# Turned down-projection with delayed scatter in a fused attention and mixture-of-experts kernel

## The chip, the cores and the metric

The kernel runs on one core of a Trainium2 chip. The metric is the device time of one execution in microseconds. A core has TensorE (PE; its weight loads are listed as PEld), VectorE (DVE), ScalarE (ACT), GpSimd (POOL) and SyncE (SP). In this kernel SP issues direct DMAs and POOL issues indirect ones (gathers and scatters); each of these engines works through its own queue in order.

## The reference

```
scores = z z^T / S                       # B = 8, S = 2496, d_qk = 64
attn   = max(scores, 0)^2
x      = u * (attn v)                    # (19968, 256) rows
logits = x @ w_gate                      # 8 experts
e      = argmax(logits)                  # one expert per row
gate   = softmax(logits)[e]
out    = gate * (max(x @ w1[e], 0) @ w2[e])   # w1: 256 x 1024, w2: 1024 x 256
```

Everything is fp32. The kernel splits each operand into a high part, in the form that PE takes (fp32r), and a low rest (hi and lo), and adds three products: hi hi, hi lo, lo hi.

## The kernel before

The first part (to about 1305 us) is attention over eight batches, five chunks of columns each. It leaves the rows x in DRAM (xrows), and for every expert a list of entries (gate and row number) in DRAM (lst), which the routing scatters there.

The second part works through tiles. A tile is a block of rows of one expert: four, three or two blocks of 128 rows. `order` holds 47 tiles, 31 of four blocks, 4 of three and 12 of two (11 further two-block tiles run only if the counts need them; with these inputs they do not). NM is 47. The last three tiles in the order have four, three and two blocks.

For each tile, by name in the code:

- `load_e` gathers the tile's entries (gate, row number) into a buffer `ent`, of which there are 6 (POOL).
- `load_x` gathers the rows x themselves, one indirect DMA per block (POOL).
- `turn_x` transposes them: DVE transposes within 32 x 32 blocks (L742), SP writes the result to DRAM (L745) and reads it back in four pieces (L747), which puts the blocks where they belong. `split_x` makes hi and lo of it (L757 on ACT, L758 on DVE).
- The hidden size 1024 is cut into 8 pieces of 128 (a two-block tile takes two pieces at once, so it has 4 groups; the others have 8). A group is one step of the loop in `tiles`.
- `up` (L775): the hidden tile of a group, six matmuls per piece, weights w1 standing, x moving, up to 512 columns. ACT takes the Relu to hh (L779), DVE makes the rest hl (L780).
- `down` (L796, L798): the rows of y. For each block s of the tile, hh[:, s] stands in PE and w2 moves, hi and lo of w2 side by side (512 columns); then hl[:, s] stands and the hi part of w2 moves (256 columns). y of a tile lies in PSUM, two blocks to a buffer of tag ps2, of which there are two; so a tile of three or four blocks takes both.
- `finish` (L806, L807, L809): per block ACT multiplies the second half of y by the gate, DVE multiplies the first half by the gate and adds; then POOL scatters the block's rows to the output.
- `load_w` gathers the weights of the next tiles' experts (POOL, L681), `split_piece` makes hi and lo of them (ACT L731 and L733, DVE L732 and L734), in rings of tag t4.

In the loop of `tiles`, `up` runs two groups ahead of `down`, and the loads three to four tiles ahead. The order of instructions on each engine is set by a planner in the tile framework, which simulates the timeline and may move instructions ahead of others. What is wrapped in `pinned(...)` comes, on each engine, behind all that was written before it. In before, `finish` is not pinned.

The buffers with the names u, x and x1 belong to the attention part (`gate_x`), one of each; after attention they are free.

Of the kernel before, what the change touches and what calls it, by code (L numbers as in the profile page):

```python
# [8 lines left out]
F32 = mybir.dt.float32  # L9
# [10 lines left out]
P = 128  # L20
KQ = 64
G, R = 4, 32
D = 256
E = 8
F = 1024
QC = 512
ENT, PAD = 16, 12
# [21 lines left out]
def fused_kernel(ctx: ExitStack, tc: tile.TileContext, zt, ut, v, wg, wcat, out):  # L49
    nc = tc.nc  # L50
# [13 lines left out]
    BS, SS = BIG // P, SMALL // P  # L64
# [3 lines left out]
    dram = ctx.enter_context(tc.tile_pool(name="dram", bufs=1, space=DRAM))  # L68
    ps2 = ctx.enter_context(tc.tile_pool(name="ps2", bufs=2, space=PSUM))
    ps1 = ctx.enter_context(tc.tile_pool(name="ps1", bufs=3, space=PSUM))  # L70
    psm = ctx.enter_context(tc.tile_pool(name="psm", bufs=1, space=PSUM))
    sb = ctx.enter_context(tc.tile_pool(name="sb", bufs=1))
# [5 lines left out]
    def ring2():  # L78
        return sb.tile([P, QC], FR, name="t2", tag="t2", bufs=10)

    def ring_f():
        return sb.tile([P, 2, QC], F32, name="tf", tag="tf", bufs=3)
# [280 lines left out]
    def pinned(work):  # L363

        last = {}
        for i in nc.cur_bb.bb.instructions[-400:]:
            last[i.engine] = i
        with ExitStack() as behind:
            for i in last.values():
                behind.enter_context(tc.issue_after(i))  # L370
            work()
# [278 lines left out]
    NF = F // P  # L650
# [12 lines left out]
    NM = len(order)  # L663
# [6 lines left out]
    blocks = [k for _, _, k in order]  # L670
# [3 lines left out]
    lists, ents, xgs, pieces, turned, xts, yts = {}, {}, {}, {}, {}, {}, {}  # L674
    outs, kept = [], []

    def load_w(w, h):
        which, t, _ = order[first_of[w]]
        wr = slot(free[0])
        free.append(free.pop(0))  # L680
        nc.gpsimd.indirect_dma_start(out=wr, out_offset=None, in_=wcat,  # L681
                                     in_offset=bass.IndirectOffsetOnAxis(ap=lists[which]["widx"][:, h, t:t + 1], axis=0))
        weights[w, h] = wr
# [2 lines left out]

    def load_e(i):
        which, t, k = order[i]
        en = ents[i] = sb.tile([P, BS, ENT], F32, name="ent", bufs=6)
        to = en.rearrange("p s w -> p (s w)")  # L690
        eidx = lists[which]["eidx"]
        parts = [(by4, t, 0, BS)] if k == BS else [(by2, t, 0, 2)]
        if k == 3:
            parts.append((lst, eidx.shape[1] - N3 + t - 2 * ND - NB, 2, 3))
        for src, at, a, z in parts:
            d = nc.gpsimd.indirect_dma_start(out=to[:, a * ENT:z * ENT], out_offset=None, in_=src,
                                             in_offset=bass.IndirectOffsetOnAxis(ap=eidx[:, at:at + 1], axis=0))
            if which == "A":
                firsts.append(d)
                for of, o in scatters:  # L700
                    if of == B - 1:
                        tc.declare_no_dep(d.ins, o.ins, reason="places of a later batch")

    def token(i, s):
        return bass.IndirectOffsetOnAxis(ap=ents[i].bitcast(I32)[:, s, 1:2], axis=0)

    def load_x(i):
        which, t, k = order[i]
        src = xrows[0:NTOK - S, :] if which == "A" else xrows
        xg = ring_rows()  # L710
        for s in range(k):
            nc.gpsimd.indirect_dma_start(out=xg[:, s, :], out_offset=None, in_=src, in_offset=token(i, s))  # L712
        xgs[i] = xg
# [37 lines left out]
    def split_x(i):  # L751

        k = blocks[i]
        tp = turned.pop(i).rearrange("p (a j t) -> p j a t", a=G, t=R)
        xh, xl = [x.rearrange("p i n -> p (i n)")[:, 0:k * D] for x in (ring_hi(), ring_lo())]
        h, l = [x.rearrange("p (j a t) -> p j a t", a=G, t=R) for x in (xh, xl)]
        nc.scalar.copy(h, tp)  # L757
        nc.vector.tensor_tensor(l, tp, h.bitcast(F32), op=ALU.subtract)  # L758
        xts[i] = [x.rearrange("p (i n) -> p i n", i=2) for x in (xh, xl)]

    def up(gi):
        i, g = groups[gi]
        n = blocks[i] * P
        w1 = pieces[piece_of[gi]][0]
        xh, xl = xts[i]
        ph = ps1.tile([P, QC], F32, name="ph", tag="ps1")
        m = fs_of[i]
        for c in range(m):
            f = g * m + c
            fs = slice(f % 2 * P, (f % 2 + 1) * P)  # L770
            o = ph[:, c * n:(c + 1) * n]
            p = 0
            for dd in range(2):
                for part, xx in ((0, xh), (0, xl), (1, xh)):
                    nc.tensor.matmul(o, lhsT=w1[:, part, dd, fs], rhs=xx[:, dd, :n], start=p == 0, stop=p == 5)  # L775
                    p += 1
        hh, hl = ring2(), ring2()
        m *= n
        nc.scalar.activation(hh[:, :m], ph[:, :m], AF.Relu)  # L779
        nc.vector.scalar_tensor_tensor(hl[:, :m], ph[:, :m], 0.0, hh[:, :m].bitcast(F32),  # L780
                                                     op0=ALU.max, op1=ALU.subtract)
        return hh, hl

    def down(gi, hh, hl):
        i, g = groups[gi]
        k = blocks[i]
        n = k * P
        w2 = pieces[piece_of[gi]][1]
        if g == 0:
            yts[i] = [ps2.tile([P, 2, QC], F32, name=f"y{s}", tag="ps2") for s in range(-(-k // 2))]  # L790
        for s in range(k):
            for c in range(fs_of[i]):
                f = g * fs_of[i] + c
                y = yts[i][s // 2][:, s % 2, :]
                cs = slice(c * n + s * P, c * n + (s + 1) * P)
                nc.tensor.matmul(y, lhsT=hh[:, cs], rhs=w2[:, f % 2].rearrange("p i d -> p (i d)"),  # L796
                                 start=f == 0, stop=False)
                nc.tensor.matmul(y[:, 0:D], lhsT=hl[:, cs], rhs=w2[:, f % 2, 0, :], start=False, stop=f == NF - 1)  # L798

    def finish(i):  # L800
        which, t, k = order[i]
        yo = ring_f().rearrange("p a (b d) -> p (a b) d", d=D)
        for s in range(k):
            y = yts[i][s // 2][:, s % 2, :]
            gate = ents[i][:, s, 0:1]
            nc.scalar.mul(yo[:, s, :], y[:, D:2 * D], gate)  # L806
            nc.vector.scalar_tensor_tensor(yo[:, s, :], y[:, 0:D], gate, yo[:, s, :], op0=ALU.mult, op1=ALU.add)  # L807
        for s in range(k):
            d = nc.gpsimd.indirect_dma_start(  # L809
                out=out, out_offset=token(i, s),  # L810
                in_=yo[:, s, :], in_offset=None, bounds_check=NTOK - 1, oob_is_err=False)
            for o in outs:
                tc.declare_no_dep(d.ins, o.ins, reason="rows are distinct")
            outs.append(d)
        del ents[i]
# [50 lines left out]
    for b in range(B):  # L866
        for c in range(NC_):
# [9 lines left out]
            f, z = {0: (-NKP * 4 + 1, 4), 1: (-NKP * 4 + 1, 4), 2: (-NKP * 4 + 1, 4), 3: (-NKP * 5 + 4, 7), 4: (-NKP * 4, 3)}[c]  # L877
# [12 lines left out]
    for work in (lambda: split_v(0, 0), lambda: split_z(0, 1), lambda: split_z(0, 2), lambda: prepare(0),  # L890
                 lambda: prepare(1), lambda: split_v(0, 1), lambda: split_z(0, 3), lambda: prepare(2)):
        pinned(work)
    bg.extend([nothing] * 2 + [constants])
    later = []
    loads = {2 * NKP - 2: [lambda: load_e(0)],
             2 * NKP - 3: [lambda: load_e(1)],
             NKP + 4: [lambda: load_x(0)],
             NKP + 3: [lambda: load_e(2)],
# [9 lines left out]
    for s, (b, c, kp) in enumerate(steps):  # L908
# [34 lines left out]
        if s == LAST:  # L943
            hs = {0: up(0)}
# [15 lines left out]

    def tiles(lo, hi, n_pieces):

        mine = [gi for gi, (i, _) in enumerate(groups) if lo <= i < hi]
        for gi in mine:
            i, g = groups[gi]
            G = NF // fs_of[i]
            if bg:
                pinned(bg.pop(0))
            if g == 0:
                for w, h in ((wof[i] + 1, 1), (wof[i] + 2, 0)):  # L970
                    if own[i] and w <= wof[hi - 1]:
                        load_w(w, h)
                if i + 3 < hi:
                    load_x(i + 3)
                if i + 4 < hi:
                    load_e(i + 4)
            ahead = min(gi + LU, mine[-1])
            while n_pieces < min(piece_of[ahead] + LP + 1, NPC * (wof[hi - 1] + 1)):
                split_piece(n_pieces)
                n_pieces += 1  # L980
            if i + 2 < hi and g == G // 2:
                turn_x(i + 2)
            if i + 1 < hi and g == G - 3:
                pinned(lambda: split_x(i + 1))
            if gi + LU <= mine[-1]:
                hs[gi + LU] = up(gi + LU)
            down(gi, *hs.pop(gi))
            if g == G - 1:
                finish(i)

    tiles(0, NM, n_pieces)
    needed = nc.values_load(lists["F"]["ns"], min_val=0, max_val=NS)

# [56 lines left out]
```

## Time and profile before

| | us |
|---|---|
| runs | 2232.24, 2224.86, 2226.58 |
| median | 2226.58 |
| profiled execution | 2225.69 |
| span of the profiled execution, first to last instruction | 2223.9 |

| engine | busy us | share of the span |
|---|---|---|
| PE | 2197.9 | 99% |
| PEld | 1854.1 | 83% |
| DVE | 1678.0 | 75% |
| ACT | 1313.2 | 59% |
| POOL | 697.4 | 31% |

All figures come from one profiled execution. Durations of matmuls overlap, since they are pipelined and their ends are modelled. The chain of waits follows the work that ended last back from the last instruction. Idle time of an engine counts only where another one waits for it.

### The profile page before, as it was taken

How to read it: one execution, taken by the hardware profiler on the slowest of the kernel's cores; microseconds unless marked ns; L12 is line 12 of the kernel's file. 1: busy time of each engine (PE TensorE's matmuls, PEld its weight loads, DVE VectorE, ACT ScalarE, POOL GpSimd, SP SyncE). 2: the span in 40 equal slices, each digit the busy share in tenths (PEclk: the TensorE clock that was granted, in tenths of full speed). 3: DMA queues.
4: the chain of work that ended last, by engine and by line, in shares of the span. 5: the costliest groups of instructions: out<-in, count | busy, mean ns of one | idle time of the engine just before them, and what ended most of it. 6: DMA issues, size and time to landing. Idle time of an engine off the chain costs nothing.

```text
span 2223.9 us, 32938 instructions
## 1 busy us (share of the span) xinstructions
PE 2197.9 (99%) x11664; PEld 1854.1 (83%) x11664; DVE 1678.0 (75%) x2782; ACT 1313.2 (59%) x1808; POOL 697.4 (31%) x720
## 2 busy tenths in 40 slices
PE   9999999999999999999999999999999999999997
PEld 6888888888888888888888888888888888888886
DVE  9888888888888888888888787566565575666653
ACT  8658657657667667667577544445454454554543
POOL 3010220220220220310222644455455455555521
PEclk9999999999999999999999999999999999999998
DMA  7966867858868758768857884565465465656530
GB/s 248 260 174 219 240 154 234 233 153 246 223 166 242 222 151 256 209 165 255 214 148 219 221 265 146 160 193 167 148 215 184 151 209 175 199 164 218 170 106 23
DMA packets 271884, 430.64 MB, mean 194 GB/s; under 512 B 109099, under 2 KB 167152, under 8 KB 252256
## 3 DMA queue, kind: packets, MB, share of 16 engines
q1 hardware_dynamic: 239200, 308.92, 48.8%
q0 software_dynamic: 32512, 119.55, 16.9%
q8 instruction: 93, 1.52, 0.3%
q14 instruction: 79, 0.65, 0.1%
HBM read 262.68 MB, written 166.20 MB: 193 GB/s over the span
## 4 chain that ended last, share of the span: by engine, by line
PE 90%; DVE 3%; DMA 2%; issue 2%; ACT 1%; POOL 1%; SPq 0%; POOLq 0%; DVEq 0%; ACTq 0%
PE ph L775 17%; PE acc L359 15%; PE acc L356 15%; PE acc L358 15%; PE y L796 12%; PE y L798 6%; PE ps_s L321 4%; PE ps_s L322 4%; PE pt L411 1%; DMA scr<-s 1%; DMA rows<-xrows,ent 1%; POOL out_dram L809 0%; POOL rows L712 0%; DVE tlo L335 0%; ACT tf L329 0%
## 5 line engine op out<-in xcount | busy, mean ns | idle before, releaser
L480 POOL DMA_INDIRECT lst<-gw,posi x160 | 201.3, 1258 | 872.0 <-DVE posi L477 535.6
L359 PE MATMUL acc<-thi,t 128*128 128x512 f32 (+1 forms) x1200 | 461.3, 386 | 0.0
L356 PE MATMUL acc<-thi,t 128*128 128x512 f32 (+1 forms) x1200 | 450.5, 386 | 0.6 <-DVE thi L333 0.6
L358 PE MATMUL acc<-tlo,t 128*128 128x512 f32 (+1 forms) x1144 | 443.0, 387 | 1.1 <-DVE tlo L335 1.1
L780 DVE SCALAR_TENSOR_TENSOR t<-ph,t 128x512 fp32r<-128x512 f32 (+1 forms) x328 | 220.0, 672 | 227.5 <-ACT t L779 223.6
L779 ACT ACTIVATE t<-ph 128x512 fp32r<-128x512 f32 (+1 forms) x328 | 192.8, 588 | 334.8 <-PE ph L775 304.2
L796 PE MATMUL y<-t,t 128*128 128x512 f32 x1062 | 378.6, 396 | 1.4 <-DVE tf L807 1.4
L775 PE MATMUL ph<-thi,t 128*128 128x512 f32 (+2 forms) x1248 | 375.6, 360 | 0.5 <-DVE t L780 0.3
L329 ACT ACTIVATE tf<-ps_s 128x1024 f32<-128x1024 f32 (+2 forms) x240 | 229.0, 962 | 184.4 <-PE ps_s L322 184.0
L798 PE MATMUL y<-t,t 128*128 128x256 f32 x1062 | 290.0, 281 | 2.6 <-DVE t L780 2.6
L356 PEld LDWEIGHTS acc<-thi,t 128*128 128x128 f32 x1200 | 225.3, 188 | 41.7 <-DVE thi L333 1.1
L359 PEld LDWEIGHTS acc<-thi,t 128*128 128x128 f32 x1200 | 225.3, 188 | 39.5
L775 PEld LDWEIGHTS ph<-thi,t 128*128 128x128 f32 x1248 | 225.5, 189 | 37.5 <-DVE t L780 1.9
L358 PEld LDWEIGHTS acc<-tlo,t 128*128 128x128 f32 x1144 | 214.9, 188 | 40.6 <-DVE tlo L335 3.4
L330 ACT ACTIVATE tf<-tf 128x1024 f32<-128x1024 f32 (+2 forms) x240 | 237.1, 998 | 5.9
L796 PEld LDWEIGHTS y<-t,t 128*128 128x128 f32 x1062 | 197.9, 188 | 43.2 <-DVE tf L807 1.9
L268 DVE STREAM_TRANSPOSE s<-tf 128x1024 f32<-128x1024 f32 x160 | 197.0, 1233 | 45.1 <-ACT tf L330 44.9
L775 PE MATMUL ph<-tlo,t 128*128 128x512 f32 (+2 forms) x624 | 224.7, 360 | 2.2 <-DVE tlo L758 2.2
L809 POOL DMA_INDIRECT out_dram<-tf,ent x160 | 166.5, 1041 | 191.6 <-DVE tf L807 151.2
L798 PEld LDWEIGHTS y<-t,t 128*128 128x128 f32 x1062 | 200.4, 189 | 13.9 <-DVE t L780 2.9
L712 POOL DMA_INDIRECT rows<-xrows,ent x160 | 164.6, 1029 | 105.1 <-DMA ent<-lst,lfeidx 60.5
L335 DVE TENSOR_TENSOR tlo<-tf,thi 128x1024 fp32r<-128x1024 f32 (+1 forms) x168 | 190.7, 1138 | 9.0 <-ACT thi L333 8.6
(237 smaller groups left out, 3929.8 us busy)
## 6 DMA issues: line engine op xcount, KB each, us to landing
scr<-s SPq DMA_DIRECT2D x80, 1024.0 KB
s<-scr SPq DMA_DIRECT2D x320, 256.0 KB
vr<-in_v_dram SPq DMA_DIRECT2D x80, 256.0 KB
u<-in_ut_dram SPq DMA_DIRECT2D x32, 512.0 KB
xrows<-th SPq DMA_DIRECT2D x128, 128.0 KB
far<-th SPq DMA_DIRECT2D x31, 512.0 KB
th<-far SPq DMA_DIRECT2D x124, 128.0 KB
lst<-pad SPq DMA_DIRECT2D x16, 624.0 KB
```

The costliest lines, as they stand in the source:

```text
L268: nc.vector.transpose(out=to, in_=a.rearrange("p i (t s k) -> p i t s k", t=4, s=G))
L329: nc.scalar.activation(a[:, :, m:n], ps[:, :, m:n], AF.Relu)
L330: nc.scalar.activation(a[:, :, m:n], a[:, :, m:n], AF.Square)
L356: nc.tensor.matmul(acc[d][:, :n], lhsT=vh, rhs=hi[:, i, :n], start=first and i == 0, stop=False)
L358: nc.tensor.matmul(acc[d][:, :n], lhsT=vh, rhs=lo[:, i, :n], start=False, stop=False)
L359: nc.tensor.matmul(acc[d][:, :n], lhsT=vl, rhs=hi[:, i, :n], start=False, stop=last and i == 1)
L480: i = nc.gpsimd.indirect_dma_start(out=lst, out_offset=bass.IndirectOffsetOnAxis(ap=posi[:m, j:j + 1], axis=0), in_=gw[:m, j, :], in_offse ...
L775: nc.tensor.matmul(o, lhsT=w1[:, part, dd, fs], rhs=xx[:, dd, :n], start=p == 0, stop=p == 5)
L779: nc.scalar.activation(hh[:, :m], ph[:, :m], AF.Relu)
L780: nc.vector.scalar_tensor_tensor(hl[:, :m], ph[:, :m], 0.0, hh[:, :m].bitcast(F32), op0=ALU.max, op1=ALU.subtract)
L796: nc.tensor.matmul(y, lhsT=hh[:, cs], rhs=w2[:, f % 2].rearrange("p i d -> p (i d)"), start=f == 0, stop=False)
L798: nc.tensor.matmul(y[:, 0:D], lhsT=hl[:, cs], rhs=w2[:, f % 2, 0, :], start=False, stop=f == NF - 1)
```

## The change

Tiles of three and four blocks, other than the last three tiles of the order, become "flat": 33 of 47.

- Their down-projection turns its operands round. For each half h of the 256 output columns the slice of w2 stands in PE and the hidden tile moves with all its columns (512 or 384): w2 hi with hh, w2 hi with hl, w2 lo with hh. y comes out with output columns on partitions and rows along the free side, and takes one ps2 buffer.
- `turn_y`, behind the tile's last group, turns it back as `turn_x` does: DVE transposes within 32 x 32 blocks from PSUM into x1, SP writes that to DRAM and reads it back in four pieces into u or x in turns.
- `finish` of a flat tile runs eight groups later, pinned: per block one multiply by the gate on ACT, then the scatters.
- There are 9 entry buffers in place of 6.

The other 14 tiles keep the form of before.

```diff
 def load_e(i):
-        en = ents[i] = sb.tile([P, BS, ENT], F32, name="ent", bufs=6)
+        en = ents[i] = sb.tile([P, BS, ENT], F32, name="ent", bufs=9)
...
+    def flat(i):
+        return blocks[i] != SS and i < NM - 3
...
         if g == 0:
-            yts[i] = [ps2.tile([P, 2, QC], F32, name=f"y{s}", tag="ps2") for s in range(-(-k // 2))]
+            if flat(i):
+                yts[i] = ps2.tile([P, 2, QC], F32, name="y", tag="ps2")
+            else:
+                y2 = [ps2.tile([P, 2, QC], F32, name=f"y{s}", tag="ps2") for s in range(-(-k // 2))]
+                yts[i] = [y2[s // 2][:, s % 2, :] for s in range(k)]
+        if flat(i):
+            for h in range(2):
+                ds_ = slice(h * P, (h + 1) * P)
+                y = yts[i][:, h, :n]
+                wh, wl = w2[:, g % 2, 0, ds_], w2[:, g % 2, 1, ds_]
+                nc.tensor.matmul(y, lhsT=wh, rhs=hh[:, :n], start=g == 0, stop=False)
+                nc.tensor.matmul(y, lhsT=wh, rhs=hl[:, :n], start=False, stop=False)
+                nc.tensor.matmul(y, lhsT=wl, rhs=hh[:, :n], start=False, stop=g == NF - 1)
+            return
...
+    def turn_y(i):
+        k = blocks[i]
+        sq = sb.tile([P, 2, QC], F32, name="x1").rearrange("p i n -> p (i n)")
+        nc.vector.transpose(out=sq[:, 0:k * D].rearrange("p (a s i e) -> p i s a e", a=G, s=k, i=2),
+                            in_=yts[i][:, :, 0:k * P].rearrange("p i (s a e) -> p i s a e", a=G, s=k))
+        far = dram.tile([P, F], F32, name="fary", tag="fary", bufs=4)
+        nc.sync.dma_start(far[:, 0:k * D], sq[:, 0:k * D])
+        tps[0] += 1
+        tp = sb.tile([P, 2, QC], F32, name="yt", tag="ux"[tps[0] % 2]).rearrange("p i n -> p (i n)")[:, 0:k * D]
+        for a in range(G):
+            nc.sync.dma_start(tp[a * R:(a + 1) * R].rearrange("p (g e) -> p g e", g=G),
+                              far[:, a * k * 2 * R:(a + 1) * k * 2 * R].rearrange("(g p) e -> p g e", g=G))
+        yts[i] = tp.rearrange("p (g s i e) -> p s i g e", g=G, s=k, i=2)
...
     def finish(i):
...
+            if flat(i):
+                nc.scalar.mul(yo[:, s, :].rearrange("p (i g e) -> p i g e", i=2, g=G), yts[i][:, s], gate)
+                continue
+            y = yts[i][s]
             nc.scalar.mul(yo[:, s, :], y[:, D:2 * D], gate)
             nc.vector.scalar_tensor_tensor(yo[:, s, :], y[:, 0:D], gate, yo[:, s, :], op0=ALU.mult, op1=ALU.add)
...
             down(gi, *hs.pop(gi))
+            if due and gi == due[0][0]:
+                pinned(lambda: finish(due.pop(0)[1]))
             if g == G - 1:
-                finish(i)
+                if flat(i):
+                    turn_y(i)
+                    due.append((gi + 8, i))
+                else:
+                    finish(i)
```

## Rows read from the trace of the kernel before

**Rows 1.** The page's part 1: busy time, share of the span, instructions of each engine.
```profile
PE 2197.9 (99%) x11664; PEld 1854.1 (83%) x11664; DVE 1678.0 (75%) x2782; ACT 1313.2 (59%) x1808; POOL 697.4 (31%) x720
```

**Rows 2.** The page's part 4, the chain that ended last, by engine and by line.
```profile
PE 90%; DVE 3%; DMA 2%; issue 2%; ACT 1%; POOL 1%; SPq 0%; POOLq 0%; DVEq 0%; ACTq 0%
PE ph L775 17%; PE acc L359 15%; PE acc L356 15%; PE acc L358 15%; PE y L796 12%; PE y L798 6%; PE ps_s L321 4%; PE ps_s L322 4%; PE pt L411 1%; DMA scr<-s 1%; DMA rows<-xrows,ent 1%; POOL out_dram L809 0%; POOL rows L712 0%; DVE tlo L335 0%; ACT tf L329 0%
```

**Rows 3.** Stretches: length; busy (x) of PE, PEld, DVE, ACT, POOL; clock; DMA share; GB/s.
```profile
400.00:600.00 200.00, 200.00 (x1056) 166.23 (x1055) 168.90 (x288) 131.72 (x153) 38.11 (x44) 1.00 0.75 212
...
1306.00:2210.00 904.00, 897.23 (x4843) 773.88 (x4842) 568.33 (x994) 442.60 (x812) 434.69 (x417) 1.00 0.53 168
```

**Rows 4.** The same stretch, first instructions on tile y alone, then line L775 alone.
```profile
1306.00:2210.00 904.00, 491.56 (x2559) 406.88 (x2560) 71.73 (x158) 71.65 (x158) 1.00 0.53 168
...
1306.00:2210.00 904.00, 488.23 (x2255) 369.40 (x2253) 1.00 0.53 168
```

**Rows 5.** Timeline of PE (start, duration): begin of 17 pairs of y, and what follows.
```profile
1849.73 0.40 PE L796 MATMUL y<-t,t 128*128 128x512 f32 x1
...
1855.74 0.40 PE L775 MATMUL ph<-thi,t 128*128 128x512 f32 x1
```

**Rows 6.** Timeline of PE: the first and the last matmul of y.
```profile
1309.67 0.61 PE L796 MATMUL y<-t,t 128*128 128x512 f32 x2
...
2210.05 0.28 PE L798 MATMUL y<-s,t 128*128 128x256 f32 x1
```

**Rows 7.** Pieces of the chain: start, length, matmuls; of 512, 512, 256 and 384 columns.
```profile
1331.92 5.46 PE ph L775 x24
...
1387.44 1.39 PE ph L775 x6
...
1438.94 2.76 PE ph L775 x23
...
2181.02 1.93 PE ph L775 x11
```

**Rows 8.** Groups of instructions, 1310 to 2224 us: busy, mean ns | idle before.
```profile
L807 DVE SCALAR_TENSOR_TENSOR tf<-y,ent,tf 128x256 f32<-128x256 f32 x160 | 72.7, 475 | 11.8 <-ACT tf L806 10.7
...
L742 DVE STREAM_TRANSPOSE th<-rows 128x1024 f32<-128x1024 f32 (+2 forms) x45 | 48.4, 1076 | 11.7 <-DMA rows<-xrows,ent 9.1 <-DMA far<-th 1.7
```

**Rows 9.** SP's timeline of one turn_x; then the stage's hardware DMA queue and gathers.
```profile
1613.16 0.34 SPq L745 DMA_DIRECT2D far<-th  x1
1615.96 1.80 SPq L747 DMA_DIRECT2D th<-far  x4
...
q1 hardware_dynamic: 34834, 40.85, 14.7%
...
rows<-xrows,ent POOLq DMA_INDIRECT x140, 3.5
```

**Rows 10.** Timeline of PE at three waits, with idle time before and releaser.
```profile
1446.96 0.50 PE L775 MATMUL ph<-tlo,t 128*128 128x512 f32 x1 [0.74 <-DVE tlo L758]
...
1628.05 0.39 PE L798 MATMUL y<-t,t 128*128 128x256 f32 x1 [2.60 <-DVE t L780]
...
1629.63 0.63 PE L775 MATMUL ph<-thi,t 128*128 128x512 f32 x1
...
1632.19 0.70 PE L796 MATMUL y<-t,t 128*128 128x512 f32 x2
...
1999.23 0.50 PE L796 MATMUL y<-t,t 128*128 128x512 f32 x1 [1.44 <-DVE tf L807]
```

**Rows 11.** Waits from 1310 to 2224 us: total us, times, longest.
```profile
POOL out_dram L809 <- DVE tf L807: 151.2, 42, 17.3
POOL ent L696 <- DMA out_dram<-tf,ent: 64.6, 19, 6.3
```

**Rows 12.** Timelines of DVE and of POOL before the long wait.
```profile
1625.58 1.25 DVE L742 STREAM_TRANSPOSE th<-rows 128x1024 f32<-128x1024 f32 x1 [5.09 <-DMA rows<-xrows,ent]
...
1612.21 0.98 POOL L696 DMA_INDIRECT ent<-lst,lfeidx  x1 [3.97 <-DMA out_dram<-tf,ent]
```

More of the change, by code (lines that the diff above doesn't have):

```diff
@@ L793, in down @@
                 f = g * fs_of[i] + c
-                y = yts[i][s // 2][:, s % 2, :]
+                y = yts[i][s]
                 cs = slice(c * n + s * P, c * n + (s + 1) * P)
@@ L798, in down @@
                 nc.tensor.matmul(y[:, 0:D], lhsT=hl[:, cs], rhs=w2[:, f % 2, 0, :], start=False, stop=f == NF - 1)
+    tps = [0]
+    def turn_y(i):
[11 more added lines that the diff above has]
+        yts[i] = tp.rearrange("p (g s i e) -> p s i g e", g=G, s=k, i=2)
     def finish(i):
@@ L803, in finish @@
         for s in range(k):
-            y = yts[i][s // 2][:, s % 2, :]
             gate = ents[i][:, s, 0:1]
+            if flat(i):
+                nc.scalar.mul(yo[:, s, :].rearrange("p (i g e) -> p i g e", i=2, g=G), yts[i][:, s], gate)
+                continue
+            y = yts[i][s]
             nc.scalar.mul(yo[:, s, :], y[:, D:2 * D], gate)
@@ L961, in tiles @@
     def tiles(lo, hi, n_pieces):
+        due = []
         mine = [gi for gi, (i, _) in enumerate(groups) if lo <= i < hi]
@@ L987, in tiles @@
             down(gi, *hs.pop(gi))
+            if due and gi == due[0][0]:
+                pinned(lambda: finish(due.pop(0)[1]))
             if g == G - 1:
-                finish(i)
+                if flat(i):
[3 more added lines that the diff above has]
+                    finish(i)
+        assert not due
+    assert blocks[NM - 1] == SS
     tiles(0, NM, n_pieces)
```

## The prediction, made before the change was run

> **What bounds the kernel now.** I read the page's busy line first: PE is busy for 99% of the span, with one weight load for each of 11664 matmuls [rows 1]. Then the chain of waits: 90% of it is PE, and 18% of the span lies on the two lines of the down-projection (L796, L798), 17% on the up-projection (L775) [rows 2]. So time is gained only where PE's own stream gets shorter or where PE waits. The table of stretches fixes the stage: the expert tiles run from 1306 to 2210 us, DVE busy for 568 of 904 us, ACT 443, POOL 435, the granted clock 1.00, the DMA engines at 0.53; behind them lies a tail of 14 us, the rest of the span [rows 3]. In the stage stand 2255 recorded matmuls of the up-projection and 2559 of y [rows 4].
>
> A busy matmul overlaps the next one, so its duration says nothing; the distance between starts does. In the stretch of y alone, 17 pairs (512 columns, then 256) take 1849.73 to 1855.74, 353.5 ns a pair [rows 5]. Over all of the stage's pairs (1280; the first and the last: [rows 6]), gaps above 0.3 us left out, the 512 is followed after 233.7 ns and the 256 after 117.0: 350.7 a pair. A 512-column matmul of the up-projection is followed after 227.5 ns in runs of 24 and 231.7 in runs of six between y's; over the stage the mean is 230. The shorter ones are followed after 174 ns (384 columns) and 120 (256) [rows 7]. This balances: a group of a four-block tile takes 6 x 230 + 4 x 350.7 = 2783 ns, and 31 tiles x 8 groups give 690 us; the four three-block tiles 67; the twelve two-block tiles 136. Together 893.5 us of the 904.6 from the first to the last matmul; 11 us are stalls.
>
> **The change, part by part.** The order rule of the kernel gives 47 tiles; 33 become flat (30 of four blocks, 3 of three).
>
> 1. PE's columns. Per group of a four-block tile y streams 4 x (512 + 256) = 3072 columns in 8 matmuls; afterwards 2 x 3 x 512 = 3072 in 6. The columns are equal; only what each matmul costs above its columns changes. Before: 4 x 350.7 = 1403 ns. After: six 512-column matmuls with weights from the same ring of weight pieces and moving data from a hidden tile, which is the shape of L775: 6 x 230 = 1380. That saves 23 ns x 240 groups = 5.5 us. For three blocks 3 x 350.7 = 1052 becomes 6 x 174 = 1044, over 24 groups 0.2 us. Ends: 227.5 (the runs of 24) gives 38 ns, 9.1 us; 233.7 (what a 512 costs in y today) gives 0.2 us. I take 230, since the new stream alternates six and six as now, and keep both ends. That wh stands still for two matmuls I count at nothing: each matmul has its own weight load today too [rows 1].
>
> The Trainium skill ("TensorE: Matmul & The Clock Gate", Back-to-back issue gap) gives a distance of columns over 2.4 GHz plus about 2.5 ns. The trace has 233.7 and 117 where that rule gives 215.8 and 109.2, so its fixed part is too small here; by its two saved fixed parts the sum would be an estimate of 1.2 us in place of 5.5, which is the second rival.
>
> 2. DVE and ACT. A flat tile loses four scalar_tensor_tensor of 475 ns on DVE and gets one transpose of 1024 elements out of PSUM; the transpose of the same size from SBUF takes 1.25 us for four blocks (L742; the group's mean of 1.08 mixes sizes) [rows 8]. Nothing shows it from PSUM. Bounds: 1.25 (no difference) and 1.9 (four reads of PSUM at 475). DVE gains 0 to 0.65 us a tile and is idle for a third of the stage [rows 3]: 0 on the path. ACT keeps four multiplies a tile, from SBUF in place of PSUM.
>
> 3. The trip through DRAM: one write of 512 KB and four reads of 128 KB per flat tile, on SP, as turn_x does today (0.34 us to issue the write, the reads issued 2.8 us after it and taking 1.8 us to issue) [rows 9]. With 3.5 us to land, which is what row gathers show and an estimate here, the chain is 1.25 + 2.8 + 1.8 + 3.5 = 9.4 us. The multiplies are due eight groups later, 8 x 2.78 = 22 us. So 13 us of slack hide it; if that is used up, ACT stands at a multiply, behind it wait the Relu of the next hidden tiles (L779), and PE two groups later. SP's queue is moved past turn_x's write, which waits for a row gather; both have about 11 us of room. Traffic: 32 MB more on the hardware queue, which today moves 40.9 MB for 14.7% of the DMA engines in the stage [rows 9], so share 0.53 becomes about 0.65. In the attention stage PE was busy for 200 of 200 us at a share of 0.75 [rows 3]: 0.
>
> 4. PSUM. A four-block y takes one buffer of the two in place of both. The next tile's y no longer waits for finish; that wait is the 1.44 us at 1999 [rows 10]. With it go the runs of up-projections at a tile's start.
>
> 5. POOL. Today scatters stand in POOL's queue waiting for DVE (151 us in 42 waits), and the entry loads wait for scatters of the tile whose buffer they reuse (65 us in 19) [rows 11]. Gathers queue behind both. At 1612 an entry load waited 3.97 us, so the gather came late, DVE stood 5.09 us at the transpose of x with the residue of a hidden tile queued behind it, and PE stood 2.60 us; right after, six 512-column matmuls take 2.56 us, 427 ns apart, the lower of the two clock levels (1.2 GHz) [rows 10, 12]. With two slow ones before them that is 8 x 0.2 us. The one event costs 2.8 + 1.6 us. With nine entry buffers and scatters whose data has long landed, these waits should go: worth 4.4 us plus the 1.6 at 1999, if nothing takes their place. The other stalls, three of about 1 us (the one at 1446 stands for them) and three smaller ones, come when DVE has weight splits, finish and split_x in one burst [rows 10]; a transpose in place of four pieces leaves them about as they are. Late next would be that burst. The instruction order comes from a planner's simulated times, so a new order makes stalls of its own. Bounds for the stalls: 11 us gained and, below nothing, 20 us lost (rival three). I take half of 4.4 + 1.6, 3 us gained.
>
> 6. The last three tiles and the 14 us tail keep their form: 0. The last flat tile's scatters (four indirect DMAs of about 1 us on POOL) [rows 12] come at the end of the tile before the last two, some 28 us before PE's end: 0.
>
> **Sum.** 2223.9 - 5.5 - 0.2 - 3 = 2215.2 us of span; 1.8 lie around it (2225.7 was the profiled execution), and the median is 0.9 above that: 2217.9, taken as 2218, 0.4% faster.
>
> **Rivals.**
> - All of it comes: 227.5 ns and no stalls. 9.1 + 11 = 20 us, 2206. For: POOL's waits are its main cause of late gathers. Against: the DVE bursts stay.
> - No change: the 233.7 ns belong to the neighbourhood and not to y's form, for the runs of six are slower than the runs of 24 too; the new matmuls cost 233.7 and stalls swap places. 2226. By that rule of the Trainium skill the time lands here as well, at an estimate of 2225.
> - Slower: the transpose at a tile's end is one undivided piece of 1.25 us or more in DVE's queue, which waits for the last y matmul; hl of the next group, split_x and the weight splits stand behind it, where they could pass between the four small pieces. Then PE waits at tile ends, about 1.1 us each as at 1446. The gain of 5.7 is eaten by five such stalls, and 12 make the kernel slower by 0.3%; at half of 33 tiles it is 17.6 - 5.7 = 12 us more, 2238. For: three of them exist today with DVE in the same burst. Against: PE is two groups (5.6 us) ahead, DVE's work per tile falls, and PE no longer needs the buffer.
>
> **How the numbers follow.** Forecast 0.50 (own range 2213 to 2222), all of it 0.14, no change 0.20, slower 0.16. About 0.3%, 6.7 us, is what a measurement of this kernel can tell from no change. Faster by more (below 2220): 0.50 x 0.75 + 0.14 = 0.52. Slower by more: 0.14, as some of the slower case stays within. Within: 0.34. The range 2207 to 2231 leaves out half of the first rival and most of the last.
>
> **What would show it.** After: distances of about 230 ns at the new down lines (227 or 234 speak for the rivals), one weight load for each matmul still, a PE count lower by 480 in the stage, DVE transposes of 1.25 to 1.4 us from y, ACT multiplies that find their data there, POOL's waits for DVE and for entry buffers nearly gone, no 3 us gap at 1625, and the stage between the first up-projection and the last y about 9 us shorter. Wrong would make it: gaps of 1 us or more at tile ends behind DVE's transpose, ACT waiting for the read-back, or another drop of the clock.

## The result: 23 us faster, and the profile after

| | before | after |
|---|---|---|
| median, us | 2225.72 (4 runs, 2224.45 to 2232.24) | 2203.20 (4 runs, 2202.72 to 2204.08) |
| ratio | | 0.9893, 95% interval 0.9874 to 0.9913 |
| span of the profiled execution | 2223.9 | 2201.6 |
| first up-projection of the expert stage to last y | 904.6 | 882.0 |

The forecast was 2218, with a range of 2207 to 2231. The direction was right; the span lost 22.3 us where the sum had 8.7, that is 2.6 times as much, and more than the rival "all of it comes" (2206).

First the page of the changed kernel: busy time and instructions of each engine.

```profile
PE 2181.2 (99%) x11184; PEld 1833.3 (83%) x11184; DVE 1664.8 (76%) x2686; ACT 1313.1 (60%) x1808; POOL 698.3 (32%) x720
```

And its chain of waits, the shares by line:

```profile
PE ph L778 20%; PE acc L359 15%; PE acc L356 15%; PE acc L358 14%; PE y L804 5%; PE y L803 5%; PE y L805 5%; PE ps_s L321 4%; PE ps_s L322 4%; PE y L812 2%; DMA scr<-s 1%; PE y L814 1%; PE pt L411 1%; DMA s<-scr 1%; DMA xrows<-th 0%
```

Against [rows 1] there are 480 matmuls less and as many weight loads less: one load for each matmul still. Next the stretch of the expert stage (length; busy of PE, PEld, DVE, ACT, POOL; clock; DMA share; GB/s), and under it, in the same columns of PE and PEld, line L778 (the up-projection, L775 before) alone.

```profile
1306.00:2188.00 882.00, 881.12 (x4365) 752.97 (x4363) 555.32 (x900) 442.80 (x813) 436.08 (x417) 1.00 0.66 210
...
1306.00:2188.00 882.00, 491.81 (x2256) 383.50 (x2254) 1.00 0.66 210
```

PE is idle for 0.9 us of 882; before it was 6.8 of 904 [rows 3]. The DMA share rose from 0.53 to 0.66. Now the distances between starts. The timeline of PE around two groups (start, duration):

```profile
1848.02 0.39 PE L778 MATMUL ph<-thi,t 128*128 128x512 f32 x1
...
1849.38 0.39 PE L803 MATMUL y<-t,t 128*128 128x512 f32 x1
...
1850.74 0.39 PE L778 MATMUL ph<-thi,t 128*128 128x512 f32 x1
...
1852.10 0.39 PE L803 MATMUL y<-t,t 128*128 128x512 f32 x1
```

Six up-projections take 1.36 us, six matmuls of y take 1.36 us: 226.7 ns each. Over the stage, distances above 0.3 us left out, the mean is 227.3 for the up-projection with 512 columns (230 before) and 227.1 for the new lines of y. A group of a four-block tile is 12 x 227.2 = 2.73 us, where it was 2.78. Then the waits of the stage (waiter, released by: total us, times, longest):

```profile
POOL out_dram L845 <- ACT tf L839: 94.3, 22, 27.5
POOL ent L696 <- DMA out_dram<-tf,ent: 59.4, 21, 6.5
```

PE's timeline again, at the one gap over 0.4 us that is left (in brackets the idle time before the matmul and what ended it):

```profile
2164.72 0.44 PE L778 MATMUL ph<-thi,t 128*128 128x384 f32 x1 [0.75 <-DVE t L783]
```

Last, DVE's transposes of y (min/median/max in ns), then the reads of the trip that brings y back (KB each, median us from issue to landing), and SP's wait for the write before them (total us, times, longest):

```profile
L822 DVE STREAM_TRANSPOSE x<-y x33: 972/1244/1252, 1332.2 to 2139.3; 128x1024 f32<-128x1024 f32 x30, 128x768 f32<-128x768 f32 x3
...
yt<-fary SPq DMA_DIRECT2D x120, 128.0 KB, 3.5
...
SPq L829 <- DMA fary<-x: 109.1, 33, 8.0
```

GpSimd waits 94 us for the multiplies, where it waited 151 us for DVE, and 59 us for entry buffers, where it was 65 [rows 11]; none of the stalls of [rows 10] is left. So the 22.7 us of the stage (904.64 - 881.97) split in two. Call excess what a distance over 0.3 us has above the mean of its kind: it came to 10.5 us before and is 1.3 now, so 9.2 us are stalls. The other 13.5 us are PE's own rate: y 1403 - 1363 = 40 ns a group x 240 groups = 9.6 us, and the up-projection of four-block tiles 31 x 48 matmuls x 2.6 ns = 3.9 us, although nothing in it was changed. These figures are of one profiled execution of each kernel.

### The profile page after: what moved, and what is told of

Same layout as the page of the kernel before. It is cut to its first block, busy times and chain, and to the rows that moved or that the text cites. A ratio compares the mean times of both kernels' runs of the same rounds, so it can differ in the third digit from the quotient of the medians.

```text
span 2201.6 us, 32033 instructions
## 1 busy us (share of the span) xinstructions
PE 2181.2 (99%) x11184; PEld 1833.3 (83%) x11184; DVE 1664.8 (76%) x2686; ACT 1313.1 (60%) x1808; POOL 698.3 (32%) x720
## 4 chain that ended last, share of the span: by engine, by line
PE 93%; DMA 3%; DVE 2%; issue 1%; ACT 1%; POOL 0%; SPq 0%; POOLq 0%; ACTq 0%; DVEq 0%
PE ph L778 20%; PE acc L359 15%; PE acc L356 15%; PE acc L358 14%; PE y L804 5%; PE y L803 5%; PE y L805 5%; PE ps_s L321 4%; PE ps_s L322 4%; PE y L812 2%; DMA scr<-s 1%; PE y L814 1%; PE pt L411 1%; DMA s<-scr 1%; DMA xrows<-th 0%
## 5 line engine op out<-in xcount | busy, mean ns | idle before, releaser
L778 PE MATMUL ph<-thi,t 128*128 128x512 f32 (+2 forms) x1248 | 379.7, 358 | 0.8 <-DVE t L783 0.8
L778 PEld LDWEIGHTS ph<-thi,t 128*128 128x128 f32 x1248 | 226.3, 188 | 35.8 <-DVE t L783 1.1
L778 PE MATMUL ph<-tlo,t 128*128 128x512 f32 (+2 forms) x624 | 222.8, 358 | 0.0
L322 PE MATMUL ps_s<-t,t 128*128 128x512 f32 (+2 forms) x480 | 178.7, 375 | 0.0
L333 ACT CAST thi<-tf 128x1024 fp32r<-128x1024 f32 (+2 forms) x162 | 158.9, 983 | 21.6 <-PE acc L359 18.8
L804 PE MATMUL y<-t,t 128*128 128x512 f32 (+1 forms) x436 | 167.8, 385 | 0.0
L805 PE MATMUL y<-t,t 128*128 128x512 f32 (+1 forms) x436 | 167.5, 384 | 0.0
```

What stands on the lines that cost most here:

```text
L322: nc.tensor.matmul(ps[:, i, m:n], lhsT=hl_k, rhs=lh_q[:, m:n], start=False, stop=True)
L804: nc.tensor.matmul(y, lhsT=wh, rhs=hl[:, :n], start=False, stop=False)
L805: nc.tensor.matmul(y, lhsT=wl, rhs=hh[:, :n], start=False, stop=g == NF - 1)
```

## The experiments

Each comparison is with the kernel before on the same chip; "stage" is the first up-projection to the last y of the profiled execution, 904.6 us before and 882.0 after.

**Why is PE faster, and why in the up-projection too?** Sorting the 512-column matmuls of before by their place behind the last narrower one gave a hint: the first behind a 256 is followed after 233 to 235 ns, the third to fifth after about 230, and from about the seventh on it is 226.7. Two theories, two kernels. In the first, no narrow matmul is left in four-block tiles and a hidden tile still stands in PE:

```diff
-  nc.tensor.matmul(y[:, 0:D], lhsT=hl[:, cs], rhs=w2[:, f % 2, 0, :], ...)
+  nc.tensor.matmul(y, lhsT=hl[:, cs], rhs=w2[:, f % 2].rearrange("p i d -> p (i d)"), ...)
```

> The kernel before, with the low part of the hidden tile also multiplied by both halves of w2, so that its 256-column matmul becomes one of 512 (one more product than needed is added). Theory A (a 256-column matmul makes the long ones behind it late): with no short ones left in four- and three-block tiles every 512 is followed after 227 ns, in y and in the up-projection: 1280 pairs x (454 - 350.7) = +132 us, up-projections 1488 x (230 - 226.7) = -5 us, about 2353 us. Theory B (a hidden tile standing in PE costs more than a weight piece standing there): y stays at 234 ns, up at 230: 1280 x (468 - 350.7) = +150 us, about 2375 us.

Measured: 2350.43 us, ratio 1.0554 (1.0533 to 1.0575). Its timeline of PE, eight matmuls of y and six of the up-projection:

```profile
1900.86 0.39 PE L796 MATMUL y<-t,t 128*128 128x512 f32 x1
...
1902.68 0.39 PE L775 MATMUL ph<-thi,t 128*128 128x512 f32 x1
...
1904.04 0.39 PE L796 MATMUL y<-t,t 128*128 128x512 f32 x1
```

1.82 us for eight and 1.36 for six: 227.5 and 226.7 ns. With hidden tiles standing the rate is that of the changed kernel, so theory B falls; A gave 2353.

In the second, the changed kernel gets narrow matmuls back, while w2 stands:

```diff
-  nc.tensor.matmul(y, lhsT=wl, rhs=hh[:, :n], ...)
+  m = n // 2 if k == BS else n
+  for q in range(0, n, m):
+      nc.tensor.matmul(yts[i][:, h, q:q + m], lhsT=wl, rhs=hh[:, q:q + m], ...)
```

> The changed kernel, with the third product (w2 low, hidden high) of four-block tiles cut into two matmuls of 256 columns: four short ones in a group, as many as before the change, but w2 still stands. Theory A: the short ones are followed after 117 ns, long ones behind them after 230 to 235, up-projections between them at about 231: 4 x 3.5 + 4 x 8 + 6 x 4 = 70 ns a group x 240 = 15 to 17 us, 2219 us. Theory B: w2 stands, so long ones stay at 227 and only the two extra matmuls per half cost something, 16 ns a group, 4 us: 2207 us.

Measured: 2210.56 us (ratio to before 0.9926, 0.9909 to 0.9942), 7.4 us over the changed kernel. The timeline of PE, the starts of y, up-projection, y and up-projection:

```profile
1851.27 0.39 PE L803 MATMUL y<-t,t 128*128 128x512 f32 x1
...
1852.65 0.40 PE L778 MATMUL ph<-thi,t 128*128 128x512 f32 x1
...
1854.02 0.39 PE L803 MATMUL y<-t,t 128*128 128x512 f32 x1
...
1855.41 0.40 PE L778 MATMUL ph<-thi,t 128*128 128x512 f32 x1
```

y takes 1.38 to 1.39 us in place of 1.36, and the up-projection between 1.37. Over the stage the two long ones behind the narrow pair are followed after 234 and 235 ns, the first two up-projections after 232, the later ones after 227. That is theory A's sign at half of its price (31 ns a group, where 70 were expected). Narrow matmuls make the wide ones behind them late; how late depends on how they are mixed.

Is it the width itself, or that a load of weights finds no room beside 256 columns? Two more kernels, both from before. One widens the narrow one to 384, the other sorts the group, wide ones first:

```diff
-  nc.tensor.matmul(y[:, 0:D], lhsT=hl[:, cs], rhs=w2[:, f % 2, 0, :], ...)
+  nc.tensor.matmul(y[:, 0:384], lhsT=hl[:, cs], rhs=w2[:, f % 2].rearrange("p i d -> p (i d)")[:, 0:384], ...)
```

```diff
-  for s in range(k):
-      for c in range(fs_of[i]):
-          ...  # 512 columns, then 256
+  for c in range(fs_of[i]):
+      for x, w in ((hh, 2), (hl, 1)):
+          for s in range(k):
+              ...  # w * 256 columns
```

> The kernel before, with the short matmul of y widened from 256 to 384 columns (part of one more product than needed is added). Theory L (a load of weights takes about 120 ns, which is the distance where 256-column matmuls follow each other, and finds no room beside a matmul of 256 columns): beside 384 there is room, so the 384 is followed after 173, the 512 after 227, up-projections of 512 after 227: 1280 x (400 - 350.7) - 4 = +59 us, 2285 us. Theory M (every change of width costs): 512 after 234, up-projections 230: 1280 x (407 - 350.7) = +72 us, 2298 us.

> The kernel before, with the matmuls of a group in another order: first all 512-column ones of its blocks, then all 256-column ones. Theory M (a change of width costs): one change in place of four, some 50 ns a group less, 248 groups: about 2214 us, long ones in y at 227 but for the first. Theory L (each short one costs its load): the short ones follow each other after 120, and the long ones behind them stay late as before in sum: 2226 us within 4.

Measured: with 384 columns 2302.94 us, ratio 1.0303 (1.0279 to 1.0328); sorted 2229.98 us, ratio 0.998 (0.9966 to 0.9993). In these two runs the kernel before was itself at 2234.55, so ratios count. The timeline of PE with 384 columns, three pairs and then six up-projections:

```profile
1904.02 0.39 PE L796 MATMUL y<-t,t 128*128 128x512 f32 x1
...
1905.25 0.40 PE L775 MATMUL ph<-thi,t 128*128 128x512 f32 x1
...
1906.65 0.39 PE L796 MATMUL y<-t,t 128*128 128x512 f32 x1
```

1.23 us are 410 ns a pair (400 would be free of it), and six up-projections take 1.40 us, 233 each. So theory L falls: a wider narrow matmul does not cure it, and the stage without its excess (980.4 - 11.1) is 75 us longer than that of before (904.6 - 10.5), where M gave 72. A group of the sorted kernel, y and then six up-projections:

```profile
1762.92 1.54 PE L797 MATMUL y<-t,t 128*128 128x512 f32 x8
1764.30 0.40 PE L775 MATMUL ph<-thi,t 128*128 128x512 f32 x1
...
1765.68 2.01 PE L797 MATMUL y<-t,t 128*128 128x512 f32 x10
```

The sorted order is some 4 us shorter by the same measure (908.9 - 18.6), not the 12 of M. In this group the four wide ones of y, which stand behind six up-projections, are followed after 226 to 227 ns, and the four narrow ones after 113, 119, 120 and 120. The delay has moved to the up-projections behind them: 233, 236, 229, 232, 231 and 227. What the runs show is that streams of one width run at 226.7 ns per 512 columns and mixed ones do not, at 256 as at 384; what in PE causes it stays open.

**Which part took the stalls away?** Three candidates: the PSUM buffer that a tile no longer takes, the entry buffers, and DVE's share of finish.

```diff
-  yts[i] = ps2.tile([P, 2, QC], F32, name="y", tag="ps2")
+  yts[i] = [ps2.tile([P, 2, QC], F32, name=f"y{h}", tag="ps2")[:, 0, :] for h in range(2)]
```

> The changed kernel, with the two halves of a flat y in a ps2 buffer each, so that a tile takes both buffers as before the change; DVE transposes each half by its own instruction. Theory C (the stalls went because a y no longer takes both buffers): the next tile's y waits for the transpose again, up-projections run ahead at a tile's start, and gaps of 0.3 to 3 us return, 4 to 10 us together: 2207 to 2213 us. Theory D (they went because finish left DVE's burst at the tile's end): no such gaps, 2203 us within 2.

Measured: 2202.67 us (ratio 0.9892, 0.9875 to 0.9908), stage 881.6. The stretch of its expert stage:

```profile
1306.00:2187.00 881.00, 880.25 (x4363) 752.44 (x4361) 555.46 (x931) 441.84 (x812) 432.34 (x417) 1.00 0.65 210
```

PE runs ahead with up-projections at a tile's start as before the change, and no gap comes back: it is idle for 0.75 us of 881. Theory C falls: the PSUM buffers were worth nothing.

```diff
-  en = ents[i] = sb.tile([P, BS, ENT], F32, name="ent", bufs=6)
+  en = ents[i] = sb.tile([P, BS, ENT], F32, name="ent", bufs=9)
```

> The kernel before, with nine entry buffers in place of six and nothing else. Theory E (the long stall at 1625 came from an entry load that waited for its buffer): the wait of GpSimd for the scatters falls to nearly nothing and the gap at 1625 with its slow-clock stretch goes, 4.4 us, perhaps 1.6 more: 2220 us. Theories C and D: gaps of the same total, 2226 us within 2.

Measured, from the kernel before: 2219.69 us, ratio 0.9966 (0.9953 to 0.9979), stage 898.8. The wait of GpSimd for scatters:

```profile
POOL ent L696 <- DMA out_dram<-tf,ent: 31.9, 12, 4.9
```

And in PE's timeline the gap that is left where [rows 10] has 1446:

```profile
1447.73 0.50 PE L775 MATMUL ph<-tlo,t 128*128 128x512 f32 x1 [0.74 <-DVE tlo L758]
```

The gap at 1625, its slow-clock stretch and the one at 1999 are gone, 5.8 us of the stage; theory E holds, although the waits only fell to half (64.6 before). Three gaps of about 1 us and the three smaller ones are all there. For those the next kernel takes DVE out of finish as well, on top of the nine buffers:

```diff
+  if k == SS:
       nc.vector.scalar_tensor_tensor(yo[:, s, :], y[:, 0:D], gate, yo[:, s, :], op0=ALU.mult, op1=ALU.add)
```

> The kernel before with nine entry buffers, and without DVE's scalar_tensor_tensor in finish for tiles of three and four blocks (the first half of y is left out of the output there). Theory F (the gaps of about 1 us that nine entry buffers left at 1446, 1525, 1655, 1713 and 1842 come from finish's four DVE pieces standing in one burst with split_x and the weight splits): the gaps fall from 5.0 us together to 1 or 2, 2215 to 2216 us against 2219.7. Theory G (split_x and the weight splits alone are too many): the gaps stay, 2219 to 2220 us.

Measured: 2215.43 us, ratio 0.9943 (0.9922 to 0.9963). The stretch of its expert stage:

```profile
1306.00:2200.00 894.00, 894.00 (x4845) 774.11 (x4844) 517.24 (x860) 439.20 (x812) 435.30 (x417) 1.00 0.53 170
```

PE is busy for 894.00 of 894 us, no distance over 0.32 us is left: theory F. So stage lengths go 904.6, 898.8 (nine buffers), 894.1 (no DVE pieces in finish), and the rest to 882.0, 12.1 us, is PE's rate (13.2) less 1.1 us of new excess.

**Do the delay, the order and the trip matter?** Five changes of the due time, of the pin and of `turn_y`, all on the changed kernel:

```diff
-  due.append((gi + 8, i))
+  due.append((gi + 2, i))      # and, in other runs, 4 and 6
```

```diff
-  pinned(lambda: finish(due.pop(0)[1]))
+  finish(due.pop(0)[1])
```

```diff
-  far = dram.tile(...); nc.sync.dma_start(far[:, 0:k * D], sq[:, 0:k * D]); ... # write and four reads
+  tp = sq[:, 0:k * D]          # DVE writes into the buffer that finish reads
```

> The changed kernel, with finish due two groups after the tile's end in place of eight. Theory H (the delay is needed, since the trip takes about 1.2 + 2.8 + 1.7 + 3.5 = 9 us and two groups are 5.4 us): ACT waits 3 to 4 us at the first multiply of each flat tile, the Relu behind it is late, PE stands 0.5 to 2 us a tile and may fall to the lower clock: 2215 to 2270 us. Theory I (the planner's lead of two groups and the hidden ring take it up): 2203 to 2206 us.

> The changed kernel, with finish of flat tiles at the same place in the text but not pinned, so that the planner may move it. Theory J (the delay in the text is enough): 2203 us within 2. Theory K (the order counts; the planner puts multiplies and scatters earlier, ahead of the read-back as it really lands, or ahead of gathers): gaps behind ACT or GpSimd, 3 us or more, 2206 to 2215 us.

> The changed kernel without the trip through DRAM: DVE transposes y into the buffer that finish reads, and the write and the four reads are left out (rows come out in the wrong places). If the trip is hidden, as the prediction has it: 2203 us within 2, no gap less. If its traffic or SP's queue costs something: 2199 us or less.

> The changed kernel, with finish due four groups after the tile's end (10.9 us). With finish due after two groups the first multiply came 8 to 17 us behind the start of DVE's transpose, since it waited for the read-back. If that length is the trip's own, half of the tiles are still late by up to 6 us; PE has two groups of lead, so it stands for 0.5 to 3 us in about a third of them and falls to the lower clock in some: 2208 to 2235 us. If the long ones came only from SP's queue waiting behind the stalls, 2203 to 2206 us.

> The changed kernel, with finish due six groups after the tile's end (16.3 us). By the lengths of 8 to 17 us nearly all read-backs have landed, and the rest lies inside PE's lead: 2203 us within 2, no gap behind ACT. If eight groups were needed: gaps as in the run with four, 2206 us or more.

| finish | median us | ratio to before, 95% | excess in PE's distances, us |
|---|---|---|---|
| two groups later | 2277.60 | 1.0222 (1.0180 to 1.0263) | 76 |
| four | 2302.45 | 1.0314 (1.0277 to 1.0352) | 97 |
| six | 2256.47 | 1.0129 (1.0106 to 1.0152) | 43 |
| eight, not pinned | 2276.66 | 1.0214 (1.0183 to 1.0246) | 71 |
| eight, without the trip | 2203.16 | 0.9885 (0.9860 to 0.9911) | 1.3 |
| eight (the change) | 2203.20 | 0.9893 (0.9874 to 0.9913) | 1.3 |

The trip is hidden: without it the stage is 882.0 us as well. The delay and the pin are not a detail. First, of the kernel with two groups, ACT's wait for the read-back:

```profile
ACT tf L839 <- DMA yt<-fary: 144.5, 31, 11.3
```

Its timeline at ACT's first late multiply and what PE does behind it:

```profile
1390.98 1.70 ACT L839 ACTIVATE tf<-yt,ent 128x256 f32<-128x256 f32 x4 [8.50 <-DMA yt<-fary]
...
1393.21 0.50 PE L803 MATMUL y<-t,t 128*128 128x512 f32 x1 [3.19 <-ACT t L782]
...
1395.38 0.63 PE L804 MATMUL y<-t,t 128*128 128x512 f32 x1
1395.81 0.63 PE L805 MATMUL y<-t,t 128*128 128x512 f32 x1
```

The same wait in the kernel that is not pinned:

```profile
ACT tf L839 <- DMA yt<-fary: 127.1, 30, 8.3
```

ACT stands 8.5 us at a multiply whose data has not come back from DRAM, the Relu of the next hidden tile stands behind it, PE waits 3.2 us, and its next matmuls are 0.43 us apart, at a granted clock of 0.50, the lower level (1.2 GHz). The kernel that is not pinned does the same at the same multiply (8.24 us): the planner had moved finish to about where the kernel with two groups has it, in most tiles three or four Relus behind the transpose in both (eight in the changed kernel). Theories H and K hold in kind, not in size: H had at most 2270, K 2215.

For the kernel with four groups, ACT's wait for the read-back, and for the one with six, a wait of ACT's Relu:

```profile
ACT tf L839 <- DMA yt<-fary: 94.2, 19, 9.5
...
ACT t L782 <- remote: 53.5, 18, 6.7
```

With four groups ACT still waits for read-backs, but the kernel is slower than with two, and far above the 2235 that was expected at most; why is not shown. With six these waits are nearly gone (5.9 us in 2), and the kernel is nevertheless 53 us behind the changed one: ACT and DVE stand for several us at a time before the next hidden tile, and the profile names no releaser ("remote", "issue"). The trace of that run holds 1112 updates of the semaphore that 1217 of PE's matmuls raise (the changed kernel's has 1221 for 1218), and those of the runs with four groups, with 384 columns and with the sorted order lack some too, so they cannot settle what was waited for. What holds ACT and DVE there stays open; the expectation of 2203 was wrong. Nor was the changed kernel itself run on the chip of these two; only the ratios link them.

## Why the prediction was wrong in size

The sum had 8.7 us, and the stage lost 22.7. Three terms were too small: y by 4.1 us, the up-projection, which was not in the sum, by 3.9, and the stalls by 6.2. The rival "all of it comes" had y (9.1) nearly right and the stalls (11) somewhat high; what it lacked was the up-projection too.

1. PE's rate in y. Predicted 23 ns a group with ends of 1 and 38; measured 40. The step that failed is the choice of 230 ns "since the new stream alternates six and six as now". The alternation was not what slowed the runs of six in [rows 7]; the 256-column matmuls before them were. 5.5 us were forecast, 9.6 came. That wh standing for two matmuls saves no load was right.
2. The up-projection was not in the sum at all. It fell from 230 to 227.3 ns and gave 3.9 us. The row that said so was there: 227.5 in runs of 24, 231.7 in runs of six [rows 7]; I read it as a bound for y, not as a price that y puts on its neighbours. The second rival read it worse still: it took the 233.7 for a property of the place.
3. By the Trainium skill ("TensorE: Matmul & The Clock Gate", Back-to-back issue gap) only two fixed parts a group were to be saved, an estimate of 1.2 us. The trace does not agree: 226.7 ns after 512 columns where that rule gives 215.8, and a surcharge behind narrow matmuls that it does not have.
4. Stalls. Predicted 3 us, half of 4.4 + 1.6; measured 9.2. The entry buffers gave all of the 6 (5.8 in the stage with nine buffers alone), so the halving was caution without a row. "A transpose in place of four pieces leaves them about as they are" failed: taking DVE's pieces out of finish shortened the stage by 4.7 us. In the changed kernel a transpose of 1.24 us stands in for the four pieces, and ACT's multiplies come eight groups later; which of the two did it there, no run separates.
5. The cause given for the wait at 1999 (PSUM) was one step short. DVE's timeline before it:

```profile
1997.18 1.25 DVE L742 STREAM_TRANSPOSE th<-rows 128x1024 f32<-128x1024 f32 x1 [1.48 <-DMA rows<-xrows,ent]
1998.35 0.83 DVE L807 SCALAR_TENSOR_TENSOR tf<-y,ent,tf 128x256 f32<-128x256 f32 x2
```

The new y did wait for finish to leave its buffer, but finish stood behind a transpose of x that waited for a late gather. Nine entry buffers alone remove the wait, with both PSUM buffers still taken, and two buffers a tile bring no gap back.
6. DVE's transpose out of PSUM (1.24 us; bounds 1.25 and 1.9), the share of the DMA engines (0.66; 0.65), the tail (13.9 us in the span before, 14.0 after) and the trip at nothing were right. The reads landed after 3.5 us as estimated (the trace has 12 of these 120), but SP waited up to 8.0 us for the write to land, where the sum had the reads 2.8 us behind it. On the four tiles whose last landing is on record the trip took 8.5 to 18.7 us from the start of the transpose, and the multiply came 2.1 to 12.6 us behind it. So the 13 us of slack were the good case, and that eight groups were enough was in part luck.
7. "POOL's waits nearly gone" was wrong: 59 us of 65 remain for the entry buffers and 94 where 151 were for the scatters. It did not matter; their total says nothing of the two events that reached PE.
8. The rival "slower" had its place wrong. DVE's undivided transpose stalled nothing; the danger was ACT's multiply in front of the Relu. The text names it and prices it at zero, which held with eight groups and the pin alone. With finish two to six groups later, or not pinned, the kernel is 28 to 74 us slower than the kernel before on the same chip, by medians.

## What to carry to other kernels

Read the distances of PE's matmuls by what came before them: a stream of one width ran at 226.7 ns per 512 columns, and narrow ones mixed in cost the wide ones behind them as well, in lines that were not touched. Before halving a stall "for caution", follow it to the buffer that it hangs on and try that buffer alone. When a result takes a trip and comes back, place its use in each engine's queue by hand behind the work that must not wait, and check that the planner has not moved it.

## What the runs showed of the hardware that was not expected

- The first 512-column matmul behind a 256-column one is followed after 233 to 235 ns, and only from about the seventh on it is 226.7; with 384 columns as the narrow width it is 234 to 236 for the first. Cause open.
- Matmuls of 256 columns next to each other are followed after 119 to 120 ns in the up-projections of two-block tiles, more than half of 226.7.
- With finish six groups later ACT and DVE stood for up to 7 us with no releaser in a profile that lacks part of the semaphore updates. Cause open.
